# Seven products of zeros ahead of the first products, and a longer stretch in which the engines keep the source's order

## The chip, the cores and the metric

The kernel runs on one core of a Trainium2 chip. The metric is the device time of one execution in microseconds (us), lower is better; where there are several executions the median counts.

## The reference: what is computed

A chunked linear recurrence over 768 positions (4 batches, 8 heads, head width 32, state width 16) gives `y`; its heads are laid side by side as 3072 tokens of width 256, and a feed-forward layer with 2048 hidden features follows:

```python
L = np.exp(cum[:, :, :, None] - cum[:, :, None, :]) * causal
y_intra = np.einsum('bhij,bhjd->bhid', (Cc @ Bc.T) * L, xc)
y_inter = np.einsum('bhin,bhnd->bhid', Cc, state) * np.exp(cum)
state = decay_full * state + sum_j(Bc_j xc_j * decay_from_j)
...
h = x @ w_in
g = np.maximum(h, 0.0) + np.log1p(np.exp(-np.abs(h)))
return g @ w_out
```

(`@` stands here for the batched products of the original.) The tokens are float32. `w_in` and `w_out` are float64 and are cut on the chip into a high and a low fp32r part.

## The kernel before, in words

The 768 positions are six units of 128 (u = 0 to 5), and each unit with its four batches is one block of 512 tokens for the feed-forward layer (j = 0 to 5). The names in the trace are these. For a unit: `sp` are the scores, products of rows of `un` (for unit 0 `head_in_h` and `head_in_l`), four PSUM tiles for each half p; `rm` holds the decay factors, written by GpSimd's `affine_select` from `fc` (`decays`, L356) and multiplied by `sp` on VectorE (`weigh`, L396); `yp` is the unit's output in PSUM, from `rm`, and from `cc` and the state `tb`; `bp` (`scale_b`, L400), `cc` (`scale_c`, L410) and `td` (`decay_state`, L438) are small VectorE products that prepare the state's step; `zp` is the state's increment; `gg` is `yp` times the growth (`grow`, L517), and `xh`, `xl` are its high and low part (L520, L524), the feed-forward layer's input. At the start the logarithms `both_logs` and the sum matrices `kc` give `fp`, whose exponentials are `fc`.

The feed-forward layer goes by steps (j, k), k = 0 to 15 being a tile of 128 hidden features. `first` makes `hp` from six products of 512 columns; `parts_of` (L608) makes `e` (softplus, ScalarE), `gh` (its high part, ScalarE) and `gl` (the rest, VectorE, L617); `second` adds six products of 512 columns to two sums `acc0` and `acc1` (PSUM, one buffer each), in the order gh, gl, gh for each. `gh` and `gl` have four buffers. `finish` (L688) adds the kept half sums and writes the outputs `o0`, `o1` (L681).

What sets the order. TensorE and the load queue always keep the order in which the source issues (`PE` and `load`). Every other engine's instruction may be moved by the framework's scheduler, unless `in_order[0]` is set while it is issued:

```python
    in_order[0] = True
...
    for word in ORDER.split():
        act(word)
...
    for s in range(AHEAD, len(steps) + LAG):
        if s == PINNED:
            in_order[0] = False
        if begins(*steps[s - LAG]):
            begin(s)
        values(s)
        begin(s)
        for word in fills[s]:
            act(word)
```

`ORDER` is an order written out by hand, of words like `D0.0.1` (a quarter of `decays`) or `P1.11` (a stage of `parts_of`). It covers units 0 to 2 and the first 32 steps. The loop behind it does step s: `second` of the step LAG = 4 before, `first` and `parts_of` of step s, then the words of `FILLS` that are due (at s = 39 those are `C@ B@.0 B@.1 T@`, that is `cc`, `bp` and `td` of unit 3). `warm(n)` (L265) makes n products of a small bf16 tile of zeros, `some`, with itself, 512 columns each, into PSUM tile `acc0`, which nobody reads; GpSimd clears `some` first of all (`constants_on_chip`). The function is there in the kernel before, and `ORDER` does not call it.

Of the kernel before, what the change touches and what calls it, by code (L numbers as in the profile page):

```python
# [55 lines left out]


ORDER = """
la loga loga ft0 logr us0.0 w0 logr gb ft0 kb S0.0 ux0.0 W0 growth gq0 us0.1 growth ux0.1 D0.0.0 W0 M0.0.0 ft0 D0.0.1
W0 M0.0.1 D0.0.2 D0.0.3 M0.0.2 M0.0.3 D0.1.0 fr0 fr0 ft0 I0.0 ft0 D1.0.2 ft0 D0.1.2 gq0 W0 B0.0 D0.1.1 S0.1 w2 B0.1 U0  # L60
G0.0 M0.1.0 gq1 fr1 M0.1.2 N0 M0.1.1 D0.1.3 M0.1.3 W0 ft1 W2 Xh0.0 fr0 D1.0.0 W0 fr1 un1.0 W2 I0.1 Xl0.0 gq1 G0.1 ft1
w4 S1.0 D1.1.0 W2 fr0 W2 D1.1.2 ft1 W4 W4 M1.0.2 ft1 Xh0.1 w1 H0 H1 fr1 un1.1 w7 Xl0.1 W4 growth D1.0.1 B1.0 W2 W2 w6
# [14 lines left out]
"""  # L77
HALF = NFT // 2
AHEAD = 32
PINNED = 34  # L80
LAG = 4
WRAW = 4
END = 4
# [27 lines left out]
def recurrence_then_ffn(ctx: ExitStack, tc: tile.TileContext, un, alr, w_in, w_out, const, outT):  # L111
# [681 lines left out]
# [3 lines that stand above are left out]
# [54 lines left out]
```

## Time and profile before

| | us |
|---|---|
| median of 3 runs | 319.69 |
| lowest, highest | 318.64, 319.97 |
| the profiled execution, its own time | 319.56 |
| its span, first to last instruction | 317.9 |
| TensorE busy (PE) | 307.7 (97%) |
| VectorE busy (DVE) | 160.9 (51%) |
| ScalarE busy (ACT) | 169.0 (53%) |
| GpSimd busy (POOL) | 38.7 (12%) |

1.66 us of the profiled execution lie outside its span. Times in the rows below are from the span's start. PE is the matmuls, PEld the loading of their weights, SPq the queue that issues loads. Matmuls are pipelined: a row's length is that of one product from its start to its end, and the distance between two starts is what a product costs in a dense stretch. In brackets stands how long the engine sat idle before the row and what ended that.

### The profile page before, as it was taken

To read this page: it belongs to the slowest core of one execution; us is meant where nothing else is said; L and a number is where in the kernel's file an instruction comes from. 1 tells how busy PE (TensorE), PEld (TensorE's weight loads), DVE (VectorE), ACT (ScalarE), POOL (GpSimd) and SP (SyncE) were. 2 spreads that over 40 slices of the span, in tenths; PEclk is the share of its full clock that TensorE was granted. 3 is DMA by queue.
4 is the path that set the end of the run, shared out by engine and by line. 5 is a ranking of instruction groups with operands and counts; after the bars stand their busy time and mean duration, and the time that the engine had idled before them with its cause. 6 is when DMAs were issued, how large, how long until landed. Compare 5 with 4: busy or idle time off the path is not lost.

```text
span 317.9 us, 5610 instructions
## 1 busy us (share of the span) xinstructions
PE 307.7 (97%) x2308; PEld 252.9 (80%) x2308; DVE 160.9 (51%) x254; ACT 169.0 (53%) x290; POOL 38.7 (12%) x47
## 2 busy tenths in 40 slices
PE   4999999999999979999999999999999999999995
PEld 4877888888888858888888788888888888888885
DVE  3999995545544863345842345462354242322222
ACT  5799899696835244433344543444533444544450
POOL 5770800000000600000600000420000000000000
PEclk9999999999999979999999999999999999999999
DMA  7957947404000531100430100000100000100001
GB/s 225 405 219 222 381 161 198 134 0 165 2 0 0 193 108 35 64 3 0 150 117 2 66 2 0 3 0 2 66 1 2 3 0 0 64 4 0 2 0 66
DMA packets 10298, 24.37 MB, mean 77 GB/s; under 512 B 1056, under 2 KB 1696, under 8 KB 10272
## 3 DMA queue, kind: packets, MB, share of 16 engines
q1 hardware_dynamic: 10272, 24.01, 22.0%
q8 instruction: 18, 0.29, 0.4%
q14 instruction: 8, 0.07, 0.1%
HBM read 20.76 MB, written 3.24 MB: 76 GB/s over the span
## 4 chain that ended last, share of the span: by engine, by line
PE 92%; DVE 5%; DMA 1%; issue 1%; ACT 1%; DVEq 0%; ACTq 0%
PE acc L131 40%; PE hp L131 40%; PE sp L131 4%; PE yp L131 4%; DVE bp L400 1%; PE fp L131 1%; PE end L131 1%; DMA both_logs<-in_alr 1%; PE zp L131 1%; DVE rm L131 1%; DVE gg L131 0%; DVE wil L131 0%; DVE w L131 0%; PE gp L131 0%; DVE half L131 0%
## 5 line engine op out<-in xcount | busy, mean ns | idle before, releaser
L617 DVE TENSOR_TENSOR gl<-e,gh 128x512 fp32r<-128x512 f32 x62 | 42.9, 691 | 100.1 <-ACT gh L614 100.1
L611 ACT ACTIVATE e<-hp 128x512 f32<-128x512 f32 x62 | 37.1, 598 | 90.5 <-PE hp L131 90.1
L131 PE MATMUL hp<-xh,wih 128*128 128x512 f32 (+1 forms) x196 | 76.2, 389 | 0.5 <-DVE rm L131 0.5
L131 PE MATMUL acc<-gl,woh 128*128 128x512 f32 x188 | 74.1, 394 | 1.9 <-DVE gl L131 1.9
L131 PE MATMUL hp<-xl,wih 128*128 128x512 f32 (+1 forms) x196 | 75.5, 385 | 0.0
L131 PE MATMUL hp<-xh,wil 128*128 128x512 f32 (+1 forms) x196 | 75.5, 385 | 0.0
L131 PE MATMUL acc<-gh,woh 128*128 128x512 f32 x188 | 74.9, 398 | 0.0
L131 PE MATMUL acc<-gh,wol 128*128 128x512 f32 x188 | 73.9, 393 | 0.0
L131 PEld LDWEIGHTS hp<-xh,wih 128*128 128x128 f32 x196 | 37.0, 189 | 8.6 <-DVE rm L131 1.0
L131 PEld LDWEIGHTS acc<-gl,woh 128*128 128x128 f32 x188 | 35.5, 189 | 9.8 <-DVE gl L131 2.7
L131 PEld LDWEIGHTS hp<-xh,wil 128*128 128x128 f32 x196 | 36.8, 188 | 7.7 <-DVE wil L131 0.3
L131 PEld LDWEIGHTS hp<-xl,wih 128*128 128x128 f32 x196 | 36.9, 188 | 7.3
L131 PEld LDWEIGHTS acc<-gh,woh 128*128 128x128 f32 x188 | 35.6, 189 | 8.7 <-issue 0.9
L131 PEld LDWEIGHTS acc<-gh,wol 128*128 128x128 f32 x188 | 35.7, 190 | 7.4
L614 ACT CAST gh<-e 128x512 fp32r<-128x512 f32 x62 | 38.5, 621 | 5.1 <-PE acc L131 3.3
L131 DVE TENSOR_TENSOR gl<-e,gh 128x512 fp32r<-128x512 f32 x34 | 22.9, 688 | 22.1 <-ACT gh L131 22.1
L131 POOL TENSOR_SCALAR_AFFINE_SELECT rm<-fc 128x512 f32<-128x512 f32 (+1 forms) x25 | 22.9, 949 | 80.0 <-PE yp L131 76.2
L131 ACT CAST gh<-e 128x512 fp32r<-128x512 f32 x34 | 20.4, 617 | 10.8 <-PE acc L131 10.6
L131 ACT ACTIVATE e<-hp 128x512 f32<-128x512 f32 x34 | 19.7, 592 | 10.8 <-PE hp L131 7.2
L131 ACT ACTIVATE signs<-wraw 128x512 f16<-128x512 f32 (+1 forms) x32 | 24.2, 783 | 0.0
L356 POOL TENSOR_SCALAR_AFFINE_SELECT rm<-fc 128x2048 f32<-128x2048 f32 x5 | 13.0, 2624 | 87.9 <-PE yp L131 87.9
L131 DVE TENSOR_TENSOR rm<-sp,rm 128x512 f32<-128x512 f32 x24 | 15.5, 683 | 6.9 <-PE sp L131 6.6
(91 smaller groups left out, 222.5 us busy)
## 6 DMA issues: line engine op xcount, KB each, us to landing
un<-in_un SPq DMA_DIRECT2D x10, 768.0 KB, 6.2
wraw<-in_w_in SPq DMA_DIRECT2D x8, 512.0 KB, 5.4
wraw<-in_w_out SPq DMA_DIRECT2D x8, 512.0 KB, 4.3
gg<-gd SPq DMA_DIRECT2D x20, 128.0 KB, 3.4
out_t<-o SPq DMA_DIRECT2D x9, 256.0 KB, 2.1
head_in_h<-in_un SPq DMA_DIRECT2D x2, 384.0 KB, 5.1
head_in_l<-in_un SPq DMA_DIRECT2D x2, 384.0 KB, 6.6
out_t<-half SPq DMA_DIRECT2D x2, 256.0 KB, 2.2
```

The lines of the kernel that those rows point to most:

```text
L131: return lambda *a, **k: tc.keep_in_program_order(f(*a, **k))
L356: Pl.affine_select(out=weights_of(u, p)[:, ks].rearrange("p h (c i) -> p (h c) i", i=SUB), in_=fs.rearrange("p h c -> p (h c)").unsqueeze( ...
L400: V.tensor_tensor(bp, home(u, p)[:, U_B:].rearrange("p (h n) -> p h n", n=N), f_tok[u][0][:, p * KP : (p + 1) * KP].unsqueeze(2).broadcast ...
L611: A.activation(e, h, AF.Softplus)
L614: A.copy(gh, e)
L617: V.tensor_tensor(gl, e, gh.bitcast(F32), op=ALU.subtract)
```

## The change

A word is added to `ORDER` behind `la`, and `PINNED` goes from 34 to 42.

```diff
 ORDER = """
-la loga loga ft0 logr us0.0 w0 logr gb ft0 kb S0.0 ...
+la warm7 loga loga ft0 logr us0.0 w0 logr gb ft0 kb S0.0 ...
...
-PINNED = 34
+PINNED = 42
```

On TensorE the only difference is fourteen instructions at the front: seven times a weight load of `some` and a product `warm<-some` of 512 columns, the first of which waits for GpSimd's clearing of `some`. The queue of loads, ScalarE and GpSimd have the same instructions in the same order as before. VectorE has the same instructions, and their order differs in three places.

The first is behind the last work of the hand-written order that adds the two kept half sums (`half1`), where unit 2's output `gg2` is made. The number behind a letter is the unit or the block, the next one the half p or the tile k; the last number is a buffer's. Before:

```order
L131 TENSOR_TENSOR half1_838<-acc1_0_1053,half1_838 128x512
L400 TENSOR_TENSOR bp3_0_1578<-un3_646,ft_90 128x256
L400 TENSOR_TENSOR bp3_1_1580<-un3_646,ft_90 128x256
L131 TENSOR_TENSOR gg2_811<-yp2_0_1239,gg2_811 128x512
L131 TENSOR_TENSOR gg2_811<-yp2_1_1240,gg2_811 128x512
L131 SCALAR_TENSOR_TENSOR tb3_1332<-zp2_1267,kb_77,td2_1173 128x4x32 x2
L410 TENSOR_TENSOR cc3_1575<-un3_646,fr_91 128x256 x2
L438 TENSOR_TENSOR td3_1582<-tb3_1332,fr_91 128x256
L131 TENSOR_TENSOR gl1_11_1343<-e1_11_1284,gh1_11_1341 128x512
L131 TENSOR_TENSOR xl_2_1346<-gg2_811,xh_2_1345 128x512
```

And with the change:

```order
L131 TENSOR_TENSOR half1_846<-acc1_0_1061,half1_846 128x512
L131 TENSOR_TENSOR gg2_819<-yp2_0_1247,gg2_819 128x512
L131 TENSOR_TENSOR gg2_819<-yp2_1_1248,gg2_819 128x512
L131 SCALAR_TENSOR_TENSOR tb3_1340<-zp2_1275,kb_77,td2_1181 128x4x32 x2
L131 TENSOR_TENSOR gl1_11_1351<-e1_11_1292,gh1_11_1349 128x512
L131 TENSOR_TENSOR xl_2_1354<-gg2_819,xh_2_1353 128x512
L131 TENSOR_TENSOR gl1_13_1361<-e1_13_1188,gh1_13_1359 128x512
L131 TENSOR_TENSOR gl1_12_1378<-e1_12_1357,gh1_12_1376 128x512
L131 TENSOR_TENSOR xl_2_1354<-gg2_819,xh_2_1353 128x512
```

Unit 3's `bp`, `cc` and `td` (five instructions) no longer stand around `gg2` and in front of `gl1_11`. They stand where the source issues them, at step 39, between `gl2_7` and `gl2_8`, on VectorE with the change:

```order
L131 TENSOR_TENSOR gl2_7_1581<-e2_7_1577,gh2_7_1579 128x512
L131 TENSOR_TENSOR cc3_1583<-un3_654,fr_91 128x256 x2
L131 TENSOR_TENSOR bp3_0_1586<-un3_654,ft_90 128x256
L131 TENSOR_TENSOR bp3_1_1588<-un3_654,ft_90 128x256
L131 TENSOR_TENSOR td3_1590<-tb3_1340,fr_91 128x256
L131 TENSOR_TENSOR gl2_8_1609<-e2_8_1605,gh2_8_1607 128x512
L131 TENSOR_TENSOR rm3_1_1543<-sp3_10_1611,rm3_1_1543 128x512
```

Before, `gl2_8` followed `gl2_7` directly. The third place is where block 1 ends, on VectorE with the change:

```order
L131 TENSOR_TENSOR gl2_1_1433<-e2_1_1429,gh2_1_1431 128x512
L131 TENSOR_TENSOR gl2_2_1452<-e2_2_1448,gh2_2_1450 128x512
L131 TENSOR_TENSOR o0_1_1460<-acc0_1_1331,half_1_1035 128x512
L131 TENSOR_TENSOR o1_1_1463<-acc1_1_1332,half_1_1035 128x512
L131 TENSOR_TENSOR gl2_3_1477<-e2_3_1473,gh2_3_1475 128x512
```

Before, `o0_1` and `o1_1` stood in front of `gl2_2`; now they stand behind it.

## Rows read from the trace of the kernel before

**Rows 1.** The chain that ended last, in order of time: start, us, what.

```profile
128.89 2.72 PE acc L131 x12
```

**Rows 2.** The waits of PE over the whole span: total us, times, longest.

```profile
PE fp L131 <- ACT both_logs L131: 4.2, 1, 4.2
PE acc L131 <- DVE gl L131: 1.9, 1, 1.9
PE hp L131 <- DVE rm L131: 0.5, 1, 0.5
```

**Rows 3.** The timeline of PE around 111 us: start, length, what.

```profile
106.03 1.10 PE L131 MATMUL yp<-cc,tb 32*64 32x128 f32 x32
...
111.05 0.39 PE L131 MATMUL acc<-gh,wol 128*128 128x512 f32 x1
111.27 0.39 PE L131 MATMUL acc<-gh,woh 128*128 128x512 f32 x1
113.61 0.50 PE L131 MATMUL acc<-gl,woh 128*128 128x512 f32 x1 [1.95 <-DVE gl L131]
...
117.33 0.63 PE L131 MATMUL acc<-gh,wol 128*128 128x512 f32 x1
117.75 0.47 PE L131 MATMUL hp<-xh,wih 128*128 128x512 f32 x1
```

**Rows 4.** Busy time by stretches; the fraction behind POOL is the granted clock.

```profile
115.00:116.00 1.00, 1.00 (x3) 0.64 (x3) 0.96 (x2) 0.51 (x1) 0.00 (x0) 0.50 0.00 0
```

**Rows 5.** The timeline of DVE around the same place.

```profile
106.32 3.92 DVE L400 TENSOR_TENSOR bp<-un,ft 128x256 f32<-128x256 f32 x2
110.16 1.28 DVE L131 TENSOR_TENSOR gg<-yp,gg 128x512 f32<-128x512 f32 x2
111.36 0.59 DVE L131 SCALAR_TENSOR_TENSOR tb<-zp,kb,td 128x128 f32<-128x128 f32 x2
111.88 0.74 DVE L410 TENSOR_TENSOR cc<-un,fr 128x256 f32<-128x256 f32 x2
112.88 0.68 DVE L131 TENSOR_TENSOR gl<-e,gh 128x512 fp32r<-128x512 f32 x1
```

**Rows 6.** The timeline of POOL around the same place.

```profile
104.93 2.53 POOL L131 TENSOR_SCALAR_AFFINE_SELECT rm<-fc 128x2048 f32<-128x2048 f32 x1 [66.18 <-PE yp L131]
107.42 2.56 POOL L356 TENSOR_SCALAR_AFFINE_SELECT rm<-fc 128x2048 f32<-128x2048 f32 x1
```

**Rows 7.** The timeline of DVE and of POOL in the first 11 us.

```profile
8.32 2.49 DVE L131 TENSOR_TENSOR rm<-sp,rm 128x512 f32<-128x512 f32 x4 [2.76 <-PE sp L131]
...
0.80 0.12 POOL L131 MEMSET some<- 128x32 bf16 x1 [0.29 <-POOLq L839]
...
6.71 3.44 POOL L131 TENSOR_SCALAR_AFFINE_SELECT rm<-fc 128x512 f32<-128x512 f32 x5 [2.14 <-ACT fc L131]
```

**Rows 8.** The timeline of ACT at 108.81 us: the cast to `gh` of k = 11.

```profile
108.81 0.62 ACT L131 CAST gh<-e 128x512 fp32r<-128x512 f32 x1 [3.83 <-PE acc L131]
```

**Rows 9.** The timeline of PE in the first 16 us.

```profile
4.21 2.00 PE L131 MATMUL fp<-both_logs,kc 128*128 128x96 f32 x8 [4.21 <-ACT both_logs L131]
6.14 2.09 PE L131 MATMUL sp<-head_in_h 32*128 32x128 f32 x32
...
11.64 1.17 PE L131 MATMUL sp<-head_in_l 32*128 32x128 f32 x32
...
14.43 1.11 PE L131 MATMUL fp<-both_logs,kc 128*128 128x96 f32 x8
```

**Rows 10.** The load of `head_in_h` issued at 1.24 us: KB, us to landing.

```profile
head_in_h<-in_un SPq DMA_DIRECT2D x1, 384.0 KB, 4.5
```

**Rows 11.** The timeline of DVE at step 39: the gap in front of one `gl`.

```profile
143.77 0.69 DVE L617 TENSOR_TENSOR gl<-e,gh 128x512 fp32r<-128x512 f32 x1 [2.02 <-ACT gh L614]
```

**Rows 12.** The end of block 1: DVE's outputs, and PE's next sum.

```profile
125.53 1.37 DVE L681 TENSOR_TENSOR o<-acc,half 128x512 f32<-128x512 f32 x2 [1.43 <-PE acc L131]
...
128.73 0.39 PE L131 MATMUL acc<-gh,woh 128*128 128x512 f32 x1
```

More of the change, by code (lines that the diff above doesn't have):

```diff
@@ L58 @@
 ORDER = """
-la loga loga ft0 logr us0.0 w0 logr gb ft0 kb S0.0 ux0.0 W0 growth gq0 us0.1 growth ux0.1 D0.0.0 W0 M0.0.0 ft0 D0.0.1
+la warm7 loga loga ft0 logr us0.0 w0 logr gb ft0 kb S0.0 ux0.0 W0 growth gq0 us0.1 growth ux0.1 D0.0.0 W0 M0.0.0 ft0 D0.0.1
 W0 M0.0.1 D0.0.2 D0.0.3 M0.0.2 M0.0.3 D0.1.0 fr0 fr0 ft0 I0.0 ft0 D1.0.2 ft0 D0.1.2 gq0 W0 B0.0 D0.1.1 S0.1 w2 B0.1 U0
```

## The prediction, made before the changed kernel was run

> **What bounds the kernel.** I read the busy times first: TensorE has 97% of the span, the next engine 53%. Then the chain of work in order of time, which is made of stretches of products one behind the other, like twelve in 2.72 us, 0.227 each [rows 1]. So the time is the stream of products, and something is to be gained only where it stands still or runs slowly. The list of TensorE's waits is short: 4.2 us before its first product, 1.9 us for one `gl`, 0.5 us for one `rm`, and 0.3 us more in the head [rows 2]. The 1.9 us wait is in the middle of the program. I then read the timelines of all engines around it, and the first 16 us, because the change touches just these two places.
>
> The middle. The stream runs dense until 111.27, one product every 0.22 us (111.05 to 111.27). The next product, with `gl` of k = 11, starts at 113.61. After that the products come every 0.42 us (117.33 to 117.75), twice the distance [rows 3]. The granted clock says why: 0.50 from 115 to 116 [rows 4]. So the engine waited 1.95 us, and its clock fell to the lower of its levels (1.2 instead of 2.4 GHz) right behind that wait.
>
> What made `gl` late is VectorE's order. At 106.32 it took the two `bp` of unit 3 and was busy with them for 3.92 us; four such products elsewhere in its row take about 0.4 us each, as the two `cc` do here (0.74 together) [rows 5]. GpSimd runs its two large `affine_select` from 104.93 to 109.98 [rows 6], and the second `bp` ends just behind that. A VectorE product of two SBUF tensors gets almost nothing done while such a select runs. One that reads PSUM is not held: four `rm<-sp` took 2.49 us, 0.62 each, under selects that ran from 6.71 to 10.15 [rows 7]. So `bp` held VectorE, and behind it stood `gg` (whose input `yp` was there at 107.13 [rows 3]), `tb`, `cc`, `td` and then `gl`, which starts at 112.88 and ends at 113.56 [rows 5].
>
> **The change, part by part.**
>
> *The longer frozen stretch.* It takes `bp`, `cc` and `td` out from in front of `gl` of k = 11. VectorE then does: `gg` from 107.2, two at 1.28; they read PSUM and are not held; ends at 108.4. `tb`, 0.59 for two [rows 5], ends at 109.0. `gl` of k = 11 needs `gh`, whose cast ends at 108.81 + 0.62 = 109.43 [rows 8]. This `gl` reads two SBUF tensors and so is held until the select ends at 109.98; at worst it starts its whole 0.68 us there and ends at 110.66. TensorE wants it one product behind 111.27, at 111.50. The margin is 0.84 us, and the wait goes.
>
> What is late next: `gl` of k = 12. Its `gh` needs the buffer that the sum of k = 10 reads until 111.05 + 0.39 = 111.44 [rows 3], so its cast ends at 112.06 and its `gl` at 112.74. `xl` and `gl` of k = 13 stand in front of it on VectorE and end at 110.66 + 2 x 0.6 = 111.9. TensorE wants it seven products behind 111.27, at 112.86. That is a margin of 0.12 us: a wait of a tenth or two may be left, far shorter than the one that went.
>
> How `tb` behaves under a select no row shows; it reads one PSUM and one SBUF tensor. Held to the end of the select it would cost 1 us on VectorE and `gl` would end near 111.3, still in time; not held, nothing. I take nothing, after the `rm<-sp` it is nearest to. The Trainium skill (GPSIMD Engine Reference, Specifications) has the SBUF interfaces contended by VectorE instructions with two SBUF inputs. By that too `tb` costs nothing, and the sum stays.
>
> The gain in the middle is read off the starts. Twelve products lie from 111.27 to the first `hp` at 117.75. At 2.72 us for twelve [rows 1] that `hp` starts at 113.99. **Gain 3.76 us**: 2.11 us of waiting and 1.65 us of slow clock.
>
> Now the clock, where a page speaks against this size. The row shows a fall to 0.50 right behind a wait of 1.95 us [rows 3, 4]. The Trainium skill (TensorE: Matmul & The Clock Gate, Why this matters for your kernels) ties such a fall to gaps between bursts longer than this one. By that rule the wait would not be the cause, the slow stretch would stay, and the middle would give 2.1 us. I go by the row, since no other gap stands near it, and keep 2.1 as the lower end.
>
> The five moved instructions now stand between two `gl` of step 39 and its neighbour, where VectorE sits idle for 2.02 us [rows 11]. They need 0.74 + 3 x 0.41 = 2.0 us, with no select running. `gl2_8` slips by at most a tenth, its sum is four steps away, and `zp` and `yp` of unit 3, which read them, come 8 us later. I cost it at nothing. The loads behind that wait for `un3` to be free wait for those `yp` in any case.
>
> `o0` and `o1` of block 1 move behind one `gl` of 0.69 us. They ended at 126.90 and would end near 128.1 against the next sum's start at 128.73 [rows 12]; the sum needs their PSUM buffers. Margin 0.6 us, cost nothing.
>
> *The seven products of zeros.* `some` is cleared by 0.92 [rows 7]; TensorE has nothing else to do until 4.21 [rows 9]. At the slow distance of 0.427 us [rows 3] seven take 2.99 us, so they run from about 1.0 to 4.0. The last one's tail of 0.63 us can touch the first `fp`; cost between 0 and 0.4 us.
>
> What they may give: the first products run at half pace. `fp` took 2.00 us at 4.21 and 1.11 us at 14.43; `sp` took 2.09 us at 6.14 and 1.17 us at 11.64 [rows 9]. The profile's clock column shows no fall there, so the paces are the evidence. Over both, 0.89 + 0.92 = 1.8 us is the most that a raised clock can return. The pace changed only after `sp`, some 4.4 us behind the first product. Counted from 1.0 instead of 4.21 that is about 5.4: half of `fp` and all of `sp` become fast. `fp` then ends at about 5.8. The first `head_in_h` lands at 1.24 + 4.5 = 5.74 [rows 10], so `sp` runs from 5.8 to 7.0 instead of to 8.23. VectorE's four `rm` waited for `sp` [rows 7] and ended at 10.81. Now they are paced by GpSimd's selects (3.44 for five, 0.69 each), which follow `fp` and start at 6.3: the last `rm` ends at 6.3 + 4 x 0.69 + 0.62 = 9.7, which is 1.1 us earlier. VectorE is almost never idle from there to the first `hp`, so most of it goes through; the loads keep their times and can hold some back. I take **0.8 us**, between 1.8 and a loss of 0.4.
>
> **The sum**, against the profiled execution's own 319.56 us (its span 317.9 and 1.66 around it): 319.56 - 3.76 - 0.8 = **315.0 us**. This execution lies 0.13 under the median of the runs, 319.69.
>
> **The rivals.** About 0.5% of the time, 1.6 us, is what can be told from no change; faster means under 318.1, slower over 321.3.
>
> 1. The zeros give nothing: the clock does not rise earlier, or the head is held by loads and by ScalarE's order. For it: the first `hp` waits for VectorE [rows 2], not for a product. Against it: `rm` waits 2.76 us for `sp`. The middle alone gives 319.56 - 3.76 = 315.8. Chance 0.14.
>
> 2. The slow stretch stays, because the wait did not cause it, or because a shorter wait left at `gl` of k = 12 still does. The middle then returns 2.1: 319.56 - 2.11 - 0.8 = 316.7. The first reason is the page's rule above. The fall's place right behind the wait speaks against it. Chance 0.08.
>
> 3. The hold only changes its victim: now `gl` of k = 11 and `xl` stand under the second select. If that select ended 0.84 us later or more, TensorE would wait again, and a wait of 2 us brings the slow clock back. The middle gives nothing: near 319.0. The selects start as `yp` frees their buffers, and the change does not touch that. Chance 0.06.
>
> 4. Slower: the frozen order at the end of block 1. `o0` and `o1` must now wait for `gl2_2`, and the next sum for them. It decides from a `gl2_2` that is 0.6 us late; a whole pair of steps late (twelve products and twelve more, 5.4 us) costs 5.4 - 0.6 = 4.8 us of waiting and 1.65 of slow clock: 315.0 + 6.45 = 321.5. For it: a frozen engine cannot go round a late input. Against it: ScalarE keeps its order, and casts the `gh` in time before. Chance 0.04.
>
> **How the numbers follow.** The forecast, both parts working, has 0.68. The time is the forecast's, 315.0. Its own bounds (the head between its ends) reach from 314.0 to 316.2; rivals 1 and 2 lie up to 316.7, and a half-left wait a little above. The range 313.9 to 317.2 leaves out rivals 3 and 4 and little else. Faster: 0.68 + 0.14 + 0.08 = 0.90; same is rival 3, 0.06; slower is rival 4, 0.04.
>
> **What would show it.** In the changed profile: TensorE's list of waits without the one for `gl`, or with one under 0.3 us; granted clock 1.00 in every stretch from 100 to 125; the first `hp` of block 2 about 4.5 us earlier than 117.75; `gl` of k = 11 ending just behind the second select; the `bp` of unit 3 at about 0.41 each. In the head: seven `warm` from about 1.0, `fp` under 2.0 us, `sp` near 1.2, the four `rm` ending near 9.7, and the first `hp` behind the 0.5 us wait 0.8 us earlier. The prediction is wrong if TensorE waits again between 103 and 125, if the clock falls there without a wait, or if `sp` still takes 2 us.

## The result, and the profile after

The changed kernel takes **315.63 us** in the median of 4 runs (314.75 to 316.49), the kernel before beside it 319.81 (318.64 to 319.97). The ratio is 0.9877, interval 0.9839 to 0.9915. The forecast was 315.0 us, with a range from 313.9 to 317.2. The profiled execution is the slowest of the four: 316.49 us, with a span of 314.8.

The busy times of the changed kernel (engine, us, share of the span, instructions):

```profile
PE 310.1 (99%) x2315; PEld 253.5 (81%) x2315; DVE 158.3 (50%) x254; ACT 169.0 (54%) x290; POOL 38.0 (12%) x47
```

TensorE now has 99% of the span, seven products more than before. Its waits in the changed kernel (total us, times, longest):

```profile
PE warm L131 <- POOL some L131: 1.0, 1, 1.0
PE sp L131 <- issue: 0.3, 1, 0.3
PE hp L131 <- DVE rm L131: 0.2, 1, 0.2
```

The wait of 1.9 us for `gl` and the one of 4.2 us in front of the first product [rows 2] are gone. The middle in the changed kernel, first TensorE's timeline (start, length of one product, what):

```profile
106.60 1.10 PE L131 MATMUL yp<-cc,tb 32*64 32x128 f32 x32
...
111.84 0.39 PE L131 MATMUL acc<-gh,woh 128*128 128x512 f32 x1
112.07 0.39 PE L131 MATMUL acc<-gl,woh 128*128 128x512 f32 x1
...
113.20 0.39 PE L131 MATMUL acc<-gh,woh 128*128 128x512 f32 x1
113.50 0.50 PE L131 MATMUL acc<-gl,woh 128*128 128x512 f32 x1
...
114.76 0.39 PE L131 MATMUL hp<-xh,wih 128*128 128x512 f32 x1
```

The product with `gl` of k = 11 stands 0.23 behind its neighbour (111.84 to 112.07), where it stood 2.34 behind [rows 3]. The one with `gl` of k = 12 stands 0.30 behind, a slip of 0.07. `yp` starts 0.57 later than before, the first `hp` of block 2 2.99 earlier (114.76 against 117.75), so over the middle TensorE won 3.56. Read at every product from 125 us on, the lead over the kernel before settles at 3.09 and stays there to the end, which makes it 3.66 (3.09 and the 0.57 by which it started late). The middle is read in this way, with settled leads, in what follows. The granted clock in the windows view of the changed kernel (stretch, length, busy times of PE, PEld, DVE, ACT and POOL, granted clock, DMA share, GB/s):

```profile
100.00:125.00 25.00, 25.00 (x224) 20.39 (x223) 12.51 (x20) 11.59 (x21) 4.88 (x2) 1.00 0.31 107
```

TensorE is busy for all of the 25 us, at a clock of 1.00 throughout. VectorE's timeline in the changed kernel, at the three places of the change:

```profile
107.73 1.29 DVE L131 TENSOR_TENSOR gg<-yp,gg 128x512 f32<-128x512 f32 x2 [0.76 <-PE yp L131]
108.94 0.60 DVE L131 SCALAR_TENSOR_TENSOR tb<-zp,kb,td 128x128 f32<-128x128 f32 x2
110.03 0.87 DVE L131 TENSOR_TENSOR gl<-e,gh 128x512 fp32r<-128x512 f32 x1 [0.49 <-ACT gh L131]
...
123.65 1.28 DVE L131 TENSOR_TENSOR o<-acc,half 128x512 f32<-128x512 f32 x2
...
139.25 0.76 DVE L131 TENSOR_TENSOR bp<-un,ft 128x256 f32<-128x256 f32 x2
139.92 0.42 DVE L131 TENSOR_TENSOR td<-tb,fr 128x256 f32<-128x256 f32 x1
140.69 0.69 DVE L131 TENSOR_TENSOR gl<-e,gh 128x512 fp32r<-128x512 f32 x1 [0.35 <-ACT gh L131]
```

And GpSimd's selects of that place, likewise in the changed kernel:

```profile
105.50 4.88 POOL L131 TENSOR_SCALAR_AFFINE_SELECT rm<-fc 128x2048 f32<-128x2048 f32 x2 [66.77 <-PE yp L131]
```

The selects end at 110.38. `tb` took its usual 0.60 under them; `gl` of k = 11, the first product of two SBUF tensors now, took 0.87 and ended at 110.90, just behind the second select. At step 39 the two `bp` take 0.76 together where no select runs, and the `gl` behind them still waits 0.35 for ScalarE. The `o` of block 1 end at 124.93.

The head of the changed kernel, on TensorE:

```profile
0.98 3.17 PE L131 MATMUL warm<-some 128*32 128x512 bf16 x7 [0.98 <-POOL some L131]
4.08 2.02 PE L131 MATMUL fp<-both_logs,kc 128*128 128x96 f32 x8
6.03 2.09 PE L131 MATMUL sp<-head_in_h 32*128 32x128 f32 x32
8.05 2.08 PE L131 MATMUL gp<-kc,logs 128*128 128x128 f32 x8
```

Here the zeros bought nothing: `fp` and `sp` take 2.02 and 2.09, as before [rows 9], and `gp` is slow as well. So this execution got all of the middle and nothing of the head; it was even 0.57 us behind the kernel before when it came to the middle. Where it fell behind is told in the last section.

### The profile page after: what moved, and what is told of

Its sections match the earlier page's. It is cut to its first block, busy times and chain, and to the rows that moved or that the text cites. A ratio compares the mean times of both kernels' runs of the same rounds, so it can differ in the third digit from the quotient of the medians.

```text
span 314.8 us, 5625 instructions
## 1 busy us (share of the span) xinstructions
PE 310.1 (99%) x2315; PEld 253.5 (81%) x2315; DVE 158.3 (50%) x254; ACT 169.0 (54%) x290; POOL 38.0 (12%) x47
## 4 chain that ended last, share of the span: by engine, by line
PE 98%; issue 0%; DVE 0%; POOL 0%; DVEq 0%; POOLq 0%
PE hp L131 42%; PE acc L131 41%; PE yp L131 5%; PE sp L131 5%; PE warm L131 1%; PE gp L131 1%; PE fp L131 1%; PE end L131 1%; PE zp L131 1%; DVE rm L131 0%; PE total L131 0%; PE rp L131 0%; DVE o_end L131 0%; PE sums L131 0%; POOL some L131 0%
## 5 line engine op out<-in xcount | busy, mean ns | idle before, releaser
L617 DVE TENSOR_TENSOR gl<-e,gh 128x512 fp32r<-128x512 f32 x54 | 37.3, 692 | 88.7 <-ACT gh L614 88.7
L131 DVE TENSOR_TENSOR gl<-e,gh 128x512 fp32r<-128x512 f32 x42 | 29.3, 707 | 33.2 <-ACT gh L131 33.1
L131 POOL TENSOR_SCALAR_AFFINE_SELECT rm<-fc 128x512 f32<-128x512 f32 (+1 forms) x26 | 24.7, 985 | 81.1 <-PE yp L131 77.4
L131 DVE TENSOR_TENSOR rm<-sp,rm 128x512 f32<-128x512 f32 x32 | 20.4, 682 | 7.1 <-PE sp L131 6.8
L356 POOL TENSOR_SCALAR_AFFINE_SELECT rm<-fc 128x2048 f32<-128x2048 f32 x4 | 10.5, 2641 | 84.4 <-PE yp L131 84.4
```

Of the source, the lines that this page charges most:

```text
L131: return lambda *a, **k: tc.keep_in_program_order(f(*a, **k))
L356: Pl.affine_select(out=weights_of(u, p)[:, ks].rearrange("p h (c i) -> p (h c) i", i=SUB), in_=fs.rearrange("p h c -> p (h c)").unsqueeze( ...
L617: V.tensor_tensor(gl, e, gh.bitcast(F32), op=ALU.subtract)
```

## The experiments

My theory was that the order on VectorE gave the middle, that the slow clock there was the long wait's consequence, and that the zeros give something in the head only when TensorE's pace rises earlier. The rivals: the middle came by some other part of the change; the clock falls there without the wait; the zeros never give anything, or give only when they fill the array.

**One part alone.** Two kernels, each with one edit of the two:

```diff
 a_freeze_only: -la warm7 loga loga
                +la loga loga
 b_zeros_only:  -PINNED = 42
                +PINNED = 34
```

> The longer frozen stretch alone, no products of zeros. Theory: the whole gain is in the middle, so this is about 315.8 us (before less 3.76), TensorE has no wait for gl near 111 us and the clock stays at 1.00 from 100 to 125 us; it equals the changed kernel within its scatter. Rival (the zeros share the gain): 316.5 or more, clearly above the changed kernel.

> The seven products of zeros alone, the stretch as before. Theory: products that fill 32 of the 128 columns do not bring the faster clock forward, so fp and sp still take about 2.0 us each and the time is that of before within 0.6 us; the 1.95 us wait for gl is there. Rival (they do help, and the profiled execution of the changed kernel was an exception): 0.8 us under before, sp near 1.2 us.

The first measured 316.15 us (6 runs, 315.97 to 316.46), ratio 0.9900, 0.9876 to 0.9925. The second measured 318.46 (12 runs, 317.48 to 319.33), ratio 0.9966, 0.9949 to 0.9982, where no gain over 0.6 was expected: the gain is 1.1, a miss. Against the 17 runs of before beside them (median 319.52) the parts are worth 3.4 and 1.1. They add up to 4.4; the changed kernel, run once more beside them with its own expectation below, has 4.3.

The second kernel also shows what I had not thought of. It has the old order and so the wait; TensorE's timeline in it:

```profile
113.71 0.50 PE L131 MATMUL acc<-gl,woh 128*128 128x512 f32 x1 [1.95 <-DVE gl L131]
...
115.00 0.39 PE L131 MATMUL acc<-gh,woh 128*128 128x512 f32 x1
115.52 0.50 PE L131 MATMUL acc<-gl,woh 128*128 128x512 f32 x1
...
116.81 0.39 PE L131 MATMUL hp<-xh,wih 128*128 128x512 f32 x1
```

And one of its windows, in the stretch where the clock of before was low:

```profile
116.00:117.00 1.00, 1.00 (x6) 0.80 (x5) 0.67 (x2) 0.00 (x0) 0.00 (x0) 1.00 0.00 0
```

The same wait of 1.95 us, and the clock stays at 1.00. The products behind it come every 0.23 to 0.24, and only the next `gl` slips (115.00 to 115.52). The middle is 1.12 us shorter than before's without any better order (10.68 us from `yp` to the first `hp` by these lines, against 11.72 [rows 3]; 1.12 once the leads have settled). So the fall is not certain. Each run's mean granted clock tells how often it comes: 0.995 in the profiled execution of before, which had the fall, and that is half speed for some 3.2 us (an estimate: 0.005 x 317.9 / 0.5).

| kernel | runs at 0.995: number, median (range) | runs at 0.998 or more |
|---|---|---|
| before, beside the first four | 10, 319.78 (319.51 to 320.48) | 7, 318.57 (318.44 to 319.00) |
| before, beside the next four | 8, 319.75 (319.54 to 320.08) | 5, 318.87 (318.40 to 319.12) |
| b_zeros_only | 5, 318.74 (318.07 to 319.33) | 7, 317.84 (317.48 to 318.55) |
| e_all_back (below) | 3, 318.80 (318.50 to 319.81) | 7, 318.45 (317.12 to 318.87) |
| the six timed kernels with a shorter wait or none (the changed one twice) | none | 34 |

In the kernel before, every run with the low mean is slower than every run without: 1.2 and 0.9 us in the medians. All runs with the fall belong to kernels with the 1.95 us wait, and 26 of their 52 runs have it. Where in those runs it lies only a profile could show; the size and the kernels fit the place behind that wait. So the freeze is worth 319.78 - 316.15 = 3.6 us against a run with the fall and 318.57 - 316.15 = 2.4 against one without. The profiles say the same: against the profile of before, which has the fall, the middle is 3.65 to 3.66 us shorter in all seven profiles with the new order, and 1.12 and 1.15 us shorter in the two that have the old order and no fall (the zeros alone, and `e_all_back` below). So the wait and what follows it cost 2.5 us without the fall, and the fall 1.1 more.

> The changed kernel itself, beside the others on the same chip. Theory: 315.6 us, with a scatter of about 1.7 us between executions that comes from when the clock rises in the first 11 us.

The changed kernel again: 315.26 us (6 runs, 314.87 to 316.37), ratio 0.9873, 0.9849 to 0.9898.

**The order put back by hand.** The changed kernel, with unit 3's instructions written into `ORDER` at their old places and left out at step 39; first all five, then the two `bp` alone:

```diff
 e_all_back: -... E0 G2.0 Z1.8 G2.1 N2 Z1.9
             +... E0 B3.0 B3.1 G2.0 Z1.8 G2.1 N2 C3 T3 Z1.9
 f_bp_back:  -... E0 G2.0
             +... E0 B3.0 B3.1 G2.0
```

> The changed kernel with unit 3's two bp put back by hand in front of gg2, and cc and td behind tb3, so that VectorE has the order of before there, all else as changed. Theory: the order of VectorE is the cause, so the wait for gl of k = 11 is back (about 2 us) and the time is that of the kernel with the zeros alone, 318 to 319 us. Rival (it is the freezing itself, or another move of it): no wait, 315.3 us.

> Only the two bp put back in front of gg2; cc and td stay at step 39. Theory: bp is held under the two selects until about 110.2, gg, tb and gl of k = 11 follow and gl ends near 112.6, so TensorE waits about 1.0 us and the clock stays at 1.00 behind so short a wait: about 316.4 us. Rival (the number of instructions in front of gl counts, not the hold: two bp are 0.8 us of work against a margin of 0.84): no wait, 315.3 us.

All five: 318.48 us (10 runs, 317.12 to 319.81), ratio 0.9966, 0.9945 to 0.9988, the level of the zeros alone. TensorE's longest wait in the middle, in the kernel with all five put back:

```profile
PE acc L131 <- DVE gl L131: 1.9, 1, 1.9
```

Its VectorE there:

```profile
106.34 3.91 DVE L131 TENSOR_TENSOR bp<-un,ft 128x256 f32<-128x256 f32 x2
...
112.90 0.68 DVE L131 TENSOR_TENSOR gl<-e,gh 128x512 fp32r<-128x512 f32 x1
```

That is the old picture to a few hundredths [rows 5], with the rest of the change in place. The two `bp` alone: 316.79 us (4 runs, 316.41 to 317.38), ratio 0.9910, 0.9896 to 0.9925; 316.4 was expected. TensorE's wait with the two `bp` put back:

```profile
PE acc L131 <- DVE gl L131: 1.1, 2, 0.9
```

And its VectorE:

```profile
106.29 3.92 DVE L131 TENSOR_TENSOR bp<-un,ft 128x256 f32<-128x256 f32 x2
...
111.84 0.67 DVE L131 TENSOR_TENSOR gl<-e,gh 128x512 fp32r<-128x512 f32 x1
```

So the two held `bp` make the first 0.9 us of the wait, and `cc` and `td` behind them, 1.06 us of VectorE's time (112.90 against 111.84), the other 1.0.

**Smaller selects under the old order.** If the hold ends with the running select, quarters must free `bp` early. The kernel before, with the selects of 2048 columns of units 3 to 5 issued in quarters; at this place that makes eight of 512 in place of two:

```diff
-    (-16, "D@.0 un@+.0 un@+.1 gg@+"),
-    (-11, "S@.0 M@.0.0 M@.0.1 M@.0.2 M@.0.3 D@.1"),
+    (-16, "D@.0.0 D@.0.1 D@.0.2 D@.0.3 un@+.0 un@+.1 gg@+"),
+    (-11, "S@.0 M@.0.0 M@.0.1 M@.0.2 M@.0.3 D@.1.0 D@.1.1 D@.1.2 D@.1.3"),
```

> The kernel before with GpSimd's selects of units 3 to 5 cut into four of 512 columns each; VectorE's order as before, no zeros. Theory: a VectorE product of two SBUF tensors is held until the select that runs ends, and gets in between two selects, so each bp takes 1 us at most instead of 1.4 and 2.6, gl is late by 0.5 us at most, and the time is 316 to 317.5 us. Rival (selects that follow each other directly leave no gap): bp is held as long as before, 319.5 us.

It measured 317.08 us (4 runs, 316.94 to 317.37), ratio 0.9919, 0.9904 to 0.9934. VectorE in that kernel:

```profile
106.34 1.26 DVE L400 TENSOR_TENSOR bp<-un,ft 128x256 f32<-128x256 f32 x2
...
109.23 1.41 DVE L410 TENSOR_TENSOR cc<-un,fr 128x256 f32<-128x256 f32 x2
110.57 0.93 DVE L438 TENSOR_TENSOR td<-tb,fr 128x256 f32<-128x256 f32 x1
111.42 0.68 DVE L131 TENSOR_TENSOR gl<-e,gh 128x512 fp32r<-128x512 f32 x1
```

Its GpSimd:

```profile
104.95 3.23 POOL L131 TENSOR_SCALAR_AFFINE_SELECT rm<-fc 128x512 f32<-128x512 f32 x4 [66.19 <-PE yp L131]
108.14 3.09 POOL L356 TENSOR_SCALAR_AFFINE_SELECT rm<-fc 128x512 f32<-128x512 f32 x4
```

The selects run a little longer in all (6.3 us to 111.2, against 5.1), but `bp` needs 1.26 us instead of 3.92. `cc` and `td` now pay too (1.41 and 0.93, against 0.74 and about 0.4 unheld), and `gl` comes at 111.42. Two waits of 0.6 us in all are left of 1.95, and no run has the low clock mean. Against the runs of before without the fall (318.87) that is 1.8 us, where the order gave 2.4 (against the runs beside it). So the hold lasts until the running select ends: the second `bp` of before ends at 110.24, 0.26 behind its select (109.98 [rows 5, 6]), and `td` here at 111.50, 0.27 behind the last of the eight (111.23). Smaller selects repair about three quarters of what the order repairs whole.

**Wider zeros.** In the late head above, seven products with weights of 32 columns changed nothing. Two kernels, the changed one with weights of all 128 columns, then the same with ones in place of zeros. Neither result is read by anyone:

```diff
-    some = ...[:, :16].bitcast(BF16)
+    some = ...[:, :64].bitcast(BF16)
...
-                w[:32].rearrange("p (a b) -> p a b", b=32),
+                w.rearrange("p (a b) -> p a b", b=128),
...
-                some.unsqueeze(1).broadcast_to([P, 16, 32]),
+                some.unsqueeze(1).broadcast_to([P, 4, 128]),
h_wide_ones, in addition:
-        Pl.memset(some, 0.0)
+        Pl.memset(some, 1.0)
```

> The changed kernel with products of zeros that fill all 128 columns (weights of 128 columns instead of 32), same number and length. Theory: it is the part of the array in use that counts, so the clock rises by about 5 us, sp takes 1.2 us, and the time is about 1 us under the changed kernel (314.6). Rival 1 (zeros never count, or the moment is chance): fp and sp stay at 2.0 us each, same time as the changed kernel.

> The changed kernel with products of 128 columns and of ones instead of zeros. Theory: what the operands hold does not matter; the clock rises as with the wide zeros, sp about 1.2 us in most executions, 315.2 us. Rival (zeros do not count as work for the clock): it rises earlier than with the zeros, 314.5 us.

TensorE's head with wide zeros:

```profile
1.06 3.17 PE L131 MATMUL warm<-some 128*128 128x512 bf16 x7 [1.06 <-POOL some L131]
4.15 1.32 PE L131 MATMUL fp<-both_logs,kc 128*128 128x96 f32 x8
5.40 1.17 PE L131 MATMUL sp<-head_in_h 32*128 32x128 f32 x32
```

With wide ones:

```profile
4.23 1.75 PE L131 MATMUL fp<-both_logs,kc 128*128 128x96 f32 x8
5.91 1.17 PE L131 MATMUL sp<-head_in_h 32*128 32x128 f32 x32
```

The profiles did what was expected: `sp` at 1.17 us. The times did not: wide zeros 315.23 us (6 runs, 314.72 to 316.43), ratio 0.9877, 0.9850 to 0.9904, the same as the changed kernel beside them (315.26), where 1 us less was expected. Wide ones 315.11 (4 runs, 314.40 to 315.49), ratio 0.9854, 0.9839 to 0.9868; that interval overlaps the changed kernel's, so neither is a better version that I can show, and zeros or ones makes no difference that I can tell.

**Two more profiles of the head.** If wide and narrow zeros take the same time, then the narrow ones must also work in most executions, and the profile after was one where they did not. The changed kernel, one profile each:

> The changed kernel once more, for a profile of another execution. Theory: the clock's rise is a matter of chance from one execution to the next, and the zeros make an early one possible: in some executions sp takes 1.2 us (clock up before 7 us), in others 2.1 us (up at 9 to 10 us). An early one stands at about 315.2 us, a late one at 316.4 us. Rival: with these zeros the clock never rises before 9 us, and the 0.9 us between the medians with and without them comes from elsewhere.

> As the look before it, another execution of the changed kernel: an early rise (sp 1.2 us, about 315.2 us) or a late one (sp 2.1 us, about 316.4 us); the rival has only the late one.

Both were of the early kind, at 314.96 and 315.22 us. TensorE's head in the first:

```profile
4.17 1.10 PE L131 MATMUL fp<-both_logs,kc 128*128 128x96 f32 x8
5.45 1.17 PE L131 MATMUL sp<-head_in_h 32*128 32x128 f32 x32 [0.17 <-DMA head_in_h<-in_un]
```

In the second:

```profile
4.17 1.43 PE L131 MATMUL fp<-both_logs,kc 128*128 128x96 f32 x8
5.52 1.17 PE L131 MATMUL sp<-head_in_h 32*128 32x128 f32 x32
```

Not all of that reaches the end. Against the profile of before the two are 1.48 and 1.18 us ahead at 31 us, and 0.98 and 0.70 at 60 us. The second loses its half microsecond at the held `gl` of the last section. The first loses it in front of one `sp`, which waits for a load of `un`, on TensorE in the first of the two:

```profile
34.79 1.17 PE L131 MATMUL sp<-un 32*128 32x128 f32 x32 [0.43 <-DMA un<-in_un]
```

So the same kernel has two heads. `sp` took 1.17 us in 3 of 7 profiles with narrow zeros (these two and the one with `bp` put back), 2.09 in the other 4, 1.17 in both with wide products (zeros and ones), and 2.09 in all 3 without any. The times show the same two levels: of the changed kernel's twelve executions nine lie from 314.75 to 315.31 and three from 315.99 to 316.49, which is the level of the freeze alone (315.97 to 316.46). The four with a profile fall in line: 314.96 and 315.22 with the early rise, 316.37 and 316.49 with the late one. What decides between the two in one execution no run here settles, nor whether full width makes the early one surer: two of the six runs with wide zeros lie at 316.3 and 316.4.

## Why the prediction was right

**The held `bp` and the `gl` behind them.** Right. The wait came back with the order and went with it. `gl` of k = 11 ended just behind the second select, as worked out, and TensorE did not wait for it.

**What is late next.** Right: a margin of 0.12 us was given for `gl` of k = 12 and "a tenth or two" left; it slips by 0.07.

**`tb` under a select.** Right as taken: 0.60 us. The page cited there (GPSIMD Engine Reference of the Trainium skill, Specifications) has the contention for VectorE instructions with two SBUF inputs; the trace agrees, with 3.92 us for two such `bp` under the selects against 0.76 without, and 0.60 for two `tb`. How long the hold lasts is the runs' own number.

**Step 39 and the outputs.** Right, both cost nothing. The lead of 3.09 us stands unchanged from 125 us to the end. Rival 4 (`o` behind `gl2_2`) would have shown in front of the next sum; that starts at 125.64 in the dense stream, behind `o` that ended at 124.93, a margin of 0.7.

**The gain of 3.76 us.** Right for the execution it was read from (3.66 measured), but it is the gain of one kind of execution. The split into 2.11 us of waiting and 1.65 us of slow clock is not what the runs show: without the fall the same wait costs 2.5, because the next `gl` is late too (115.00 to 115.52 with the zeros alone), and the fall adds 1.1. The step "its clock fell to the lower of its levels (1.2 instead of 2.4 GHz) right behind that wait" is right as a sequence and was taken as a rule; 12 of 30 runs of the kernel before have no fall, and there the freeze gives 2.4. That the profiled execution and the median of before both have the fall was luck for the forecast. Rival 2's number, 2.1 for the wait alone, is near what those executions give, by another reason than the one stated: not that the slow stretch stays, but that before did not have it either. The page of the Trainium skill weighed there (TensorE: Matmul & The Clock Gate, Why this matters for your kernels) puts such a fall behind longer gaps. The runs do not agree: no run of a kernel without the 1.95 us wait had the fall, and 26 of 52 runs with it did. So the wait belongs to the fall, and is not enough for it; what else it takes stays open.

**The zeros' 0.8 us.** Right in size over many runs, in part by luck, and wrong in its step. In medians they are worth 0.9 us (316.15 to 315.26) under the new order and 0.7 to 1.0 under the old one (318.57 to 317.84 without the fall, 319.78 to 318.74 with it; 0.4 and 0.9 in the kernel with all five put back). The step that failed is "the pace changed only after `sp`, some 4.4 us behind the first product. Counted from 1.0 instead of 4.21 that is about 5.4". No fixed delay holds: with the same seven products the pace was up by 4.2 in one execution, near 6 in another, and in the profile after only behind `gp`, near 10. The median is an early execution's, as nine of twelve are early. The head then wins more than the 1.1 us worked out (1.48 and 1.18 at 31 us in the two profiles; 0.3 in the kernel with `bp` put back, whose pace rose near 6), and half a microsecond is lost again by 60 us. The prediction had named loads that hold some back, without a size, and had no held `gl` there; that the two errors nearly cancel is the luck. A late head gives nothing, or less than nothing: at 60 us the freeze alone is 0.20 behind the profile of before, and the two late profiles of the changed kernel are 0.57 and 0.42 behind it. By the prediction's own sign, "if `sp` still takes 2 us", the head's part failed in the profile after. Rival 1 holds for that execution, and not for the median.

## What to carry to other kernels

When an engine takes far longer for an instruction than its neighbours do for the same shape, look at what the other engines run at that time, and then move what can wait out of that stretch; cutting the other engine's long instruction shorter was the weaker repair here (1.8 us against 2.4). Under such a stretch, VectorE instructions that read one operand from PSUM went at their usual speed here (0.60 us for two `tb`, 1.29 for two `gg`). And before a clock change in one profile is priced, look at the mean granted clock of all runs: what falls or rises by chance is worth its share of the runs, not what one profile shows.

## What the runs showed that I had not expected

The fall of the clock behind a wait of 1.95 us comes in 18 of 30 runs of the kernel before, 8 of 22 of two kernels with the same wait, and none of 34 runs whose longest such wait was 0.9 us or less. The rise in the head comes early or late with the same instructions in front of it.

And the same hold costs a little at a second place, in three of the four profiles of the changed kernel and not in the one of before. Near 31 us GpSimd issues eight selects of 512 columns (the changed kernel):

```profile
31.22 7.50 POOL L131 TENSOR_SCALAR_AFFINE_SELECT rm<-fc 128x512 f32<-128x512 f32 x8 [9.10 <-PE yp L131]
```

VectorE in the changed kernel:

```profile
34.66 1.25 DVE L131 TENSOR_TENSOR gl<-e,gh 128x512 fp32r<-128x512 f32 x1 [0.33 <-ACT gh L131]
```

And with the freeze alone:

```profile
34.76 0.69 DVE L131 TENSOR_TENSOR gl<-e,gh 128x512 fp32r<-128x512 f32 x1 [0.31 <-ACT gh L131]
```

The one select of the eight that starts with this `gl`, in the changed kernel:

```profile
34.67 0.72 POOL L131 TENSOR_SCALAR_AFFINE_SELECT rm<-fc 128x512 f32<-128x512 f32 x1
```

And with the freeze alone:

```profile
34.78 1.25 POOL L131 TENSOR_SCALAR_AFFINE_SELECT rm<-fc 128x512 f32<-128x512 f32 x1
```

So one of the two holds the other. Where `gl` is held it takes 1.25 us instead of 0.69; where it is not, the select takes 1.25 instead of 0.72. Which it is goes with a few nanoseconds: `gl` starts 3 to 12 ns ahead of the select in the four profiles where it was held, and 15 to 27 ns ahead in the other eight. Through the `rm` behind a held `gl` TensorE's `hp` waits 0.2 and starts 0.5 later. It was held in the profile after, in that of the same kernel run again, in the second of the two further profiles, and with the wide zeros. It takes back half a microsecond of what an early head wins, or adds it to what a late one lacks: of the 0.57 us by which the profile after was behind at the middle, 0.49 came here.
